# A state-space scan fused with a gated feed-forward layer: the first block's decays spread through four row groups of the array, and its dummy matmuls cut small

## The chip, the cores and the metric

The kernel runs on one core of one Trainium2 chip. The metric is the device time of the program in microseconds, as the median of several runs. Before the change it is 363.76 us (three runs, 362.59 to 363.86). The parts of the core are named as in the profile: PE is the matmul array (TensorE), PEld its weight loads, DVE is VectorE, ACT is ScalarE, POOL is GpSimd, and SP is SyncE, which here only issues transfers. A name with q behind it (SPq, ACTq) is the engine's instruction queue.

## The reference

Inputs: x (4 batches, 8 heads, 768 positions, 32 channels), decays a (4, 8, 768), B and C (4, 8, 768, 16), and three weight matrices. The first part is a chunked linear scan with a state of 16 by 32 for each batch and head; the second is a gated feed-forward layer on the result.

```python
log_a = np.log(np.clip(a, 1e-06, 1.0))
for c in range(nc):
    cum = np.cumsum(la, axis=-1)
    L = np.exp(cum[:, :, :, None] - cum[:, :, None, :]) * causal
    M = np.einsum('bhin,bhjn->bhij', Cc, Bc) * L
    y_intra = np.einsum('bhij,bhjd->bhid', M, xc)
    y_inter = np.einsum('bhin,bhnd->bhid', Cc, state) * np.exp(cum)[:, :, :, None]
    y[:, :, sl] = y_intra + y_inter
    state = decay_full[:, :, None, None] * state + np.sum(Bx, axis=2)
x = y.transpose(0, 2, 1, 3).reshape(3072, 256)
g = x @ w_gate
out = (g / (1 + np.exp(-g)) * (x @ w_val)) @ w_out
```

## The kernel before

**Tiling.** The 768 positions are cut into six blocks of 128 positions for all four batches at once (512 tokens a block), and each block into two pieces (q) of 64 positions, which are the scan's chunks. For each block k the kernel makes the decays L[k] (128 partitions are piece and position j; columns are batch, head and 65 positions i), the decays E[k] for the carried state, the scores S, the mixed matrix M (S times L, written over L), the sums st for the new state, the values y, and the state T. Then y is the input of the feed-forward layer: gate and value products gv in 12 steps of 128 columns of the hidden layer, silu and product (sg), and the output product po. Block 0 runs its gv in full float32 (two matmul records for one matmul, as for all float32 matmuls here); later blocks use weights split in a high and a low part, which VectorE and ScalarE make from the raw 64-bit weights during block 0 (tiles wg0 to wg11, wo0 to wo5: r raw, w rounded, h high, l low).

**Decays of block 0.** For blocks 1 to 5 the decays are clipped by GpSimd for all blocks at once, written to DRAM and loaded back with a broadcast. Block 0 cannot wait for that. `load_rows` (L239) loads its decays as 8 rows of 520 columns (rows[:, 0] for L, 8 rows that are piece and batch; rows[:, 1] for E, 8 rows that are heads). VectorE clips both (`clip_rows`, L298). `spread` (L303) copies the right rows to all 128 partitions with a float32 matmul by a matrix of zeros and ones, pick (loaded from `sel`, L876 to L879, one 8 x 128 matrix for each of the four batches and one for E). A spread covers half the columns (260), so there are eight for L and two for E; each writes a bank of PSUM in the pool `ps_at`, and VectorE scans it from there into L or E (`scan_spread`, L309), multiplying along the positions. The scan starts anew where the tile dj (for E: dn) has a one; dj is copied from the constants `cs` by ScalarE.

**What follows in block 0.** The scores (`scores_of`, L364) need C with heads kept apart (Cz, ScalarE). They are 32 small float32 matmuls on pieces of the array, 32 rows by 64 columns, and write four banks of the pool `ps_mm`. VectorE weighs B by the decays (`weigh_b`, tile xb) and mixes S with L (`mix`). PE then runs the sums st (`sums_of_pieces`), the values y (`values`, two groups of four heads), and the carried products (`carried`, tile y from bc and T). VectorE and ScalarE copy y to xf, and the first gv starts.

**Dummies.** `idle` (L621) issues a matmul of the tile unit (ones, bfloat16, 128 x 384) into a PSUM tile rest that nobody reads: eight before the first spread, eight before the carried products and eight between these and the first gv. Each has its own weight load.

**What sets the order.** Every step is added to a planner (`Plan`, L44) with an engine, a cost, a rank and what it needs; the planner runs through its own clock and issues each engine's instructions in the order it finds. `plan.follow` (L822 to L827) pins part of block 0's order by hand. The engines' queues are strictly in that order; `Ordered` (L182) pins it in the program. DMA issues sit in the queues of SP and ACT: SP issues rows, pick, the inputs of the clipping (tile all), the raw weights and later loads; ACT issues cs, then bc (B and C, 512 KB) and xb (x and B, 768 KB) of block 0.

Of the kernel before, what the change touches and what calls it, by code (L numbers as in the profile page):

```python
# [9 lines left out]
F32 = mybir.dt.float32  # L10
F32R = mybir.dt.float32r
BF16 = mybir.dt.bfloat16
# [31 lines left out]
class Plan:  # L44
# [156 lines left out]
def scan_moe_kernel(ctx: ExitStack, tc, aj, an, bc, xb, wgv, wo, cst, sel, out):  # L201
    nc = tc.nc
    PSUM = bass.MemoryType.PSUM
    te, ve, se, ge, sp = (
        Ordered(tc, e) for e in (nc.tensor, nc.vector, nc.scalar, nc.gpsimd, nc.sync)
    )

    def pool(name, bufs, stack=ctx, **kw):
        return stack.enter_context(tc.tile_pool(name=name, bufs=bufs, **kw))

    const = pool("const", 1)
    wts = pool("wts", 1)
    att = pool("att", 1)
    moe = pool("moe", 2)
    raw = pool("raw", RAW)
    dram = pool("dram", 1, space=bass.MemoryType.DRAM)
    ps_mm = pool("ps_mm", 4, space=PSUM)
    ps_at = pool("ps_at", 4, space=PSUM)

    cs = const.tile([P, CST], F32, name="cs")  # L220
    eye, hm, blk = cs[:, 0:W], cs[:, W : W + 2], cs[:, W + 2 : W + 2 + 2 * D]
    dj = const.tile([P, H, W], F32, name="dj")
    dn = const.tile([P, BATCH * K, W], F32, name="dn")
    unit = const.tile([P, 3 * P], BF16, name="unit")
    pick = const.tile([H, BATCH + 1, P], F32, name="pick")

    const.tile([P, 48], F32, name="gap")
    att.tile([P, 16], F32, name="gap2")
# [1 line left out]
    bl = [dict(y={}) for _ in range(NB)]  # L230
# [7 lines left out]

    def load_rows():  # L239

        t = moe.tile([H, 2, T + 32], F32, tag="xl", name="rows")
        t = bl[0]["rows"] = t[:, :, : H * W]
        sp.dma_start(t[:, 0], aj[0].rearrange("q (b c) -> (q b) c", b=BATCH))
        sp.dma_start(t[:, 1], an[0])

    def load_aj(k):
        t = bl[k]["L"]
# [14 lines left out]
    def new_decays(k):  # L262
        bl[k]["L"] = att.tile([P, BATCH * H, W], F32, tag="L", name=f"L{k}")
        bl[k]["E"] = att.tile([P, BATCH, K, W], F32, tag="E", name=f"E{k}")
# [22 lines left out]
    def clip(t):  # L287
        ve.tensor_scalar(t, t, 1e-6, 1.0, ALU.max, ALU.min)
# [7 lines left out]
        ve.tensor_tensor_scan(t, t, d, 0.0, ALU.mult, ALU.add)  # L296

    def clip_rows(i):  # L298
        clip(bl[0]["rows"][:, i].rearrange("p (g t) -> p g t", t=W)[:, :, 1:])

    HALF = H // 2 * W

    def spread(b, i):  # L303

        t = bl[0]["spread", b, i] = ps_at.tile([P, HALF], F32, tag="at", name=f"a{b}_{i}")
        r = bl[0]["rows"][:, b // BATCH, HALF * i : HALF * i + HALF]
        te.matmul(t, pick[:, b], r, start=True, stop=True)

    def scan_spread(b, i):  # L309
        if b < BATCH:  # L310
# [72 lines left out]
    def last(k, q):  # L383
        return k == NB - 1 and q == K - 1
# [82 lines left out]
    xh, xl = {}, {}  # L467
# [151 lines left out]
    rest = {}  # L619

    def idle(n, i):  # L621

        if not i:
            rest[n] = ps_at.tile([P, 3 * P], F32, tag="at", name=f"rest{n}")
        te.matmul(rest[n], unit[:, :P], unit, start=True, stop=True)


    load_rows()
    se.dma_start(cs, cst)
    sp.dma_start(pick, sel)  # L630
    new_decays(0)
    warm = const.tile([P, 1], F32, name="warm")
    ve.memset(unit, 1.0)
    ve.memset(warm, 1.0)
    se.activation(warm, warm, AF.Silu)
    load_bc(0)
# [4 lines left out]
    def do(f, *a):  # L641
        return lambda *e: f(*a, *e)
# [6 lines left out]
    add = plan.add  # L649

    GV, PO, ATT, FIRST, PACE0 = 2.82, 1.41, 5.0, 16.0, 3.5
    begin, begin_sum, t = {}, {}, FIRST
# [7 lines left out]
    def due(k, f=0):  # L660

        return begin[k] + f * (GV if k else PACE0)

    def due_sum(k, f):
        return begin_sum[k] + f * PO
# [5 lines left out]

    for n, ranks in enumerate(IDLE):
        for i, r in enumerate(ranks):
            need = [("idle", n, i - 1)] if i else IDLE_AFTER[n]
            takes = [] if i else [("at", ("rest", n))]
            add("PE", 0.16, do(idle, n, i), r, need, takes=takes, uses=[("rest", n)], gives=("idle", n, i), kind="r")


    for i in range(NW):
        r = due(0, i) - 1.0 if i < NF else due_sum(0, 2 * (i - NF)) - 1.0  # L680
# [7 lines left out]
        if i < NF:  # L688
            r = due(1, i) - LATER
# [10 lines left out]
    for k in range(NB):  # L700
        r = due(k)
# [9 lines left out]
        q = ("SP", 0.48) if k else ("-", 0.0)  # L711
# [7 lines left out]
        if not k:  # L719
            add("-", 0.0, lambda: None, -9, takes=[("x", "rows")], gives="rows", lag=0.2)  # L720
            for i in range(2):
                add("DVE", 0.35, do(clip_rows, i), -9 + i, ["rows"], gives=("clip", i))
            for b in range(BATCH + 1):
                r = z + 0.5 + b if b < BATCH else -1.3
                for i in range(2):
                    t = ("spread", b, i)
                    add("PE", 0.45, do(spread, b, i), r + 0.5 * i, [("clip", b // BATCH), "pick"], takes=[("at", t)], uses=[t, "rows"], gives=t, kind="s")
                    need = [t, ("decays", 0), "dj"] + ([("scan0", b)] if i else [])
                    done = ("scan0", b) if not i else ("L", 0, b) if b < BATCH else ("E", 0)
                    add("DVE", 0.63, do(scan_spread, b, i), r + 0.5 * i, need, uses=[t], gives=done)  # L730
        else:
            add("SP", 0.96, do(load_aj, k), FETCH["aj"] if k == 1 else z - 12, ["written", ("decays", k), *late], gives=("aj", k), lag=4.3)
            add("SP", 0.48, do(load_an, k), FETCH["an"] if k == 1 else z - 9, ["written", ("decays", k), *late], gives=("an", k), lag=1.1)
            for b in range(BATCH):
                add("DVE", 1.14, do(scan_j, k, b), z + 0.5 + b, [("aj", k)], gives=("L", k, b), slack=1.0)
            add("DVE", 1.17, do(scan_n, k), z + 6, [("an", k)], gives=("E", k), slack=1.0)
# [27 lines left out]
        for g in range(0 if k else 2):  # L764
            need = [("M", 0, p) for p in (2 * g, 2 * g + 1)]
# [22 lines left out]
    for k in range(NB):  # L788
        xs = [(t, k, i) for t in ("xh", "xl") for i in range(2 * K)]
        for f in range(NF):  # L790
            r = due(k, f)
            need = [*xs, ("wh", f), ("wl", f)]
            c = 1.4
            if not k:
                need = [("round", f), *(("xf", i) for i in range(2 * K))]
                c = 1.72
# [11 lines left out]
        for n, (m, t, fs) in enumerate(sums_of(k)):  # L808
            b = ("po", k, m, t)
            need = [x for f in fs for x in (("hl", k, f), ("wh", NF + f // 2), ("wl", NF + f // 2))]  # L810
            need += [prev] if prev else []
            prev = (*b, fs)
            r = due_sum(k, fs[0]) + n * 0.01
            c = 0.7 * len(fs) * (t[1] - t[0]) / T
            add("PE", c, do(project, k, m, t, fs), r, need, takes=[] if fs[0] else [("mm", b)], uses=[b, *(("h", k, f) for f in fs)], gives=prev, kind="r")
            if fs[-1] == NF - 1:
                o = ("ob", k, m, t)
                c = 0.6 * (t[1] - t[0]) / T
                add([("Act", c), ("DVE", c)], None, do(drain, k, m, t), r + 0.5, [prev], takes=[("ob", o)], uses=[b, o], gives=o)
                add("SP", 0.48, do(store, k, m, t), r + 2, [o], uses=[o], gives=("stored", k, m, t), lag=0.9)  # L820
    halves = [(b, i) for b in range(BATCH) for i in range(2)]
    plan.follow([  # L822
        *(("spread", b, i) for b, i in halves), *(("S", 0, b) for b in range(BATCH)),
        *(("spread", BATCH, i) for i in range(2)), *(("st", 0, b) for b in range(BATCH)), ("idle", 1, 0),
    ])
    plan.follow([("raw", i) for i in range(NW)])
    plan.follow([("L", 0, b) if i else ("scan0", b) for b, i in halves] + [("M", 0, p) for p in range(NP)] + [("scan0", BATCH), ("E", 0), ("ce", 0)])  # L827
# [1 line left out]
    plan.issue()  # L829


CST = W + 2 + 2 * D
NA = NB * K * BATCH * H // P
IDLE = [-9.0] * 8, [-1.2 + 0.1 * i for i in range(8)], [0.5 + 0.5 * i for i in range(8)]
IDLE_AFTER = [], [("S", 0, BATCH - 1)], [("y", 0)]
FETCH = dict(aj=10.0, an=29.0, bc=12.0, xb=31.0)
LATER = 3.0
LEAD = {1: -30.0, 2: -44.0, 3: -44.0}
# [54 lines left out]
```

## Time and profile before

| what | value |
|---|---|
| median of three runs | 363.76 us |
| the profiled execution, own time | 362.51 us |
| its span in the profile | 360.7 us |
| PE busy | 353.0 us (98%) |
| DVE busy | 238.6 us (66%) |
| ACT busy | 115.7 us (32%) |
| instructions | 7359 |

The time of the profiled execution is 1.8 us longer than its span, for what lies around the profiled instructions. Start times are counted from the span's start. The chain of waits follows the work that ended last backwards from the last instruction; "issue" in it is time in which the engine waited for nothing that the profile shows. In timeline rows the columns are start, length, engine, line (always the helper's, L190), operation, output and inputs, shapes, count, and in brackets the idle time before and what ended it. A matmul is shown with rows*columns of the array that it uses. In a tile's rows the three durations are the shortest, the median and the longest in ns. Rows of DMA queues give packets, MB and the share of 16 engines' time; rows of DMA issues give KB and the median time from issue to landing.

### The profile page before, as it was taken

What the parts mean: (1) busy time and instruction counts of PE and PEld (TensorE: products, weight loads), DVE (VectorE), ACT (ScalarE), POOL (GpSimd) and SP (SyncE); (2) the same over time, 40 slices, a digit from 0 to 9 for tenths busy, and PEclk for the clock granted to TensorE, in tenths of its full rate; (3) what the DMA queues carried; (4) which work ended last, traced back from release to release, by engine and by line L of the source; (5) the groups of instructions that cost most, each with busy time, mean ns of one, the idle gap of its engine ahead of it and who ended that gap; (6) DMA issues with size and microseconds to landing.
All of it is one profiled execution on the core that took longest, in us unless ns stands there. A gap on an engine that the chain in (4) does not pass through costs nothing.

```text
span 360.7 us, 7359 instructions
## 1 busy us (share of the span) xinstructions
PE 353.0 (98%) x3184; PEld 268.8 (75%) x3184; DVE 238.6 (66%) x446; ACT 115.7 (32%) x209; POOL 2.3 (1%) x7
## 2 busy tenths in 40 slices
PE   7989999999999999999999999999999999999996
PEld 4744444588878788887888887788877788888895
DVE  4869999989999967568263868255768250466230
ACT  3168575541353540222130322140313130311221
POOL 2000000000000000000000000000000000000000
PEclk9999999999999999999999999999999999999999
DMA  7928933290000085100056100046100000100001
GB/s 252 355 83 208 404 142 109 61 211 24 2 0 4 5 202 147 58 3 0 4 160 135 59 2 2 2 144 152 59 2 2 2 2 0 58 2 0 0 2 58
DMA packets 8456, 28.09 MB, mean 78 GB/s; under 512 B 976, under 2 KB 1872, under 8 KB 7784
## 3 DMA queue, kind: packets, MB, share of 16 engines
q1 hardware_dynamic: 7992, 26.25, 24.5%
q10 hardware_dynamic: 432, 1.38, 1.1%
q8 instruction: 25, 0.41, 0.4%
q14 instruction: 7, 0.06, 0.1%
HBM read 24.28 MB, written 3.35 MB: 77 GB/s over the span
## 4 chain that ended last, share of the span: by engine, by line
PE 90%; DVE 7%; issue 2%; DMA 1%; SPq 0%; ACT 0%; DVEq 0%; ACTq 0%
PE gv L190 51%; PE po L190 28%; PE y L190 4%; PE a L190 3%; PE S L190 2%; DVE L L190 1%; PE st L190 1%; DVE sg L190 1%; PE rest L190 1%; DMA pick<-in_sel 1%; DVE wg9w L190 1%; DVE wg7w L190 1%; DVE wg8w L190 1%; DVE T L190 1%; DVE wg5w L190 0%
## 5 line engine op out<-in xcount | busy, mean ns | idle before, releaser
L190 DVE TENSOR_TENSOR sg<-gv,sg 128x512 f32<-128x512 f32 x72 | 49.7, 690 | 69.1 <-PE gv L190 68.3
L190 ACT ACTIVATE sg<-gv 128x512 f32<-128x512 f32 x72 | 43.0, 597 | 111.9 <-PE gv L190 111.8
L190 DVE TENSOR_TENSOR hh<-sg,hh 128x512 fp32r<-128x512 f32 x72 | 49.4, 692 | 12.1 <-ACT hh L190 10.7
L190 ACT CAST hh<-sg 128x512 fp32r<-128x512 f32 x39 | 24.1, 622 | 37.1 <-PE po L190 15.2
L190 DVE TENSOR_TENSOR_SCAN L<-L,dj 128x520 f32<-128x520 f32 x20 | 23.8, 1228 | 14.1 <-DMA L<-clipped 14.1
L190 ACT COPY ob<-po 128x512 f32<-128x512 f32 (+1 forms) x13 | 7.2, 555 | 48.6 <-PE po L190 48.2
L190 DVE TENSOR_TENSOR L<-S,L 128x512 f32<-128x512 f32 x24 | 15.4, 688 | 1.5 <-PE S L190 1.5
L190 PE MATMUL po<-hh,wo0h 128*128 128x512 f32 (+1 forms) x52 | 15.7, 385 | 0.0
L190 PE MATMUL po<-hh,wo5h 128*128 128x512 f32 (+1 forms) x52 | 15.2, 375 | 0.0
L190 PE MATMUL po<-hh,wo2h 128*128 128x512 f32 (+1 forms) x52 | 15.2, 375 | 0.0
L190 PE MATMUL po<-hh,wo3h 128*128 128x512 f32 (+1 forms) x52 | 15.2, 375 | 0.0
L190 PE MATMUL po<-hh,wo4h 128*128 128x512 f32 (+1 forms) x52 | 15.1, 373 | 0.0
L190 PE MATMUL po<-hh,wo1h 128*128 128x512 f32 (+1 forms) x52 | 15.1, 373 | 0.0
L190 DVE CAST hh<-sg 128x512 fp32r<-128x512 f32 x33 | 14.1, 428 | 1.0
L190 PEld LDWEIGHTS y<-L,xb 64*32 64x32 f32 x768 | 9.1, 111 | 6.3 <-issue 3.6
L190 PE MATMUL y<-L,xb 64*32 64x64 f32 x768 | 11.1, 238 | 1.8 <-issue 1.8
L190 PEld LDWEIGHTS po<-hh,wo4h 128*128 128x128 f32 x52 | 9.5, 188 | 1.7
L190 PEld LDWEIGHTS po<-hh,wo1h 128*128 128x128 f32 x52 | 9.5, 188 | 1.7
L190 PEld LDWEIGHTS po<-hh,wo2h 128*128 128x128 f32 x52 | 9.4, 188 | 1.8
L190 PEld LDWEIGHTS po<-hh,wo3h 128*128 128x128 f32 x52 | 9.4, 188 | 1.8
L190 PEld LDWEIGHTS po<-hh,wo5h 128*128 128x128 f32 x52 | 9.4, 188 | 1.7
L190 PEld LDWEIGHTS po<-hh,wo0h 128*128 128x128 f32 x52 | 9.2, 188 | 2.0 <-issue 0.2
(272 smaller groups left out, 722.0 us busy)
## 6 DMA issues: line engine op xcount, KB each, us to landing
L<-clipped SPq DMA_DIRECT2D x10, 520.0 KB, 8.3
xb<-in_xb SPq DMA_DIRECT2D x5, 768.0 KB, 10.4
out<-ob SPq DMA_DIRECT2D x11, 256.0 KB, 2.0
bc<-in_bc SPq DMA_DIRECT2D x5, 512.0 KB, 3.4
E<-clipped SPq DMA_DIRECT2D x5, 260.0 KB
xb<-in_xb ACTq DMA_DIRECT2D x1, 768.0 KB
bc<-in_bc ACTq DMA_DIRECT2D x1, 512.0 KB, 4.2
wg0r<-in_wgv SPq DMA_DIRECT2D x1, 512.0 KB, 7.8
```

Of the source, the lines that this page charges most:

```text
L190: ins = getattr(self.engine, name)(*a, **k)
```

## The change

The four batches' rows of L are put at partitions 0, 32, 64 and 96 (two rows each, for the two pieces), so that each batch's spread uses a row group of its own. The rest of these 128 rows is filled with ones by VectorE ahead of the load, which is now two transfers, one for each piece. The matrix that spreads them is the same for all batches; it lies in 128 more columns of the constants `cs` (the view pick). Only E keeps a small matrix of its own, pick_n. The four first halves go to the banks of `ps_mm` (which the scores use after them), the four second halves to `ps_at`. A dummy is now 64 columns instead of 384, and each planned dummy step issues four: 40 before the first spreads, 24 between the first and the second halves, 28 before the carried products, 32 before the first gv. Costs and the pinned order follow.

```diff
-    unit = const.tile([P, 3 * P], BF16, name="unit")
-    pick = const.tile([H, BATCH + 1, P], F32, name="pick")
+    pick = cs[:, CST - P :]
+    unit = const.tile([P, P], BF16, name="unit")
+    pick_n = const.tile([H, P], F32, name="pick_n")
...
-        t = moe.tile([H, 2, T + 32], F32, tag="xl", name="rows")
+        t = moe.tile([P, 2, T + 32], F32, tag="xl", name="rows")
         t = bl[0]["rows"] = t[:, :, : H * W]
-        sp.dma_start(t[:, 0], aj[0].rearrange("q (b c) -> (q b) c", b=BATCH))
-        sp.dma_start(t[:, 1], an[0])
+        ve.memset(t[:, 0], 1.0)
+        to = t[:, 0].rearrange("(b r) c -> b r c", b=BATCH)
+        for q in range(K):
+            sp.dma_start(to[:, q], aj[0, q].rearrange("(b c) -> b c", b=BATCH))
+        sp.dma_start(t[:H, 1], an[0])
...
     def spread(b, i):
-        t = bl[0]["spread", b, i] = ps_at.tile([P, HALF], F32, tag="at", name=f"a{b}_{i}")
-        r = bl[0]["rows"][:, b // BATCH, HALF * i : HALF * i + HALF]
-        te.matmul(t, pick[:, b], r, start=True, stop=True)
+        where, tag = (ps_mm, "mm") if first(b, i) else (ps_at, "at")
+        t = bl[0]["spread", b, i] = where.tile([P, HALF], F32, tag=tag, name=f"a{b}_{i}")
+        half = slice(HALF * i, HALF * i + HALF)
+        if b < BATCH:
+            own = slice(32 * b, 32 * b + K)
+            te.matmul(t, pick[own], bl[0]["rows"][own, 0, half], start=True, stop=True)
+        else:
+            te.matmul(t, pick_n, bl[0]["rows"][:H, 1, half], start=True, stop=True)
...
-            rest[n] = ps_at.tile([P, 3 * P], F32, tag="at", name=f"rest{n}")
-        te.matmul(rest[n], unit[:, :P], unit, start=True, stop=True)
+            rest[n] = ps_at.tile([P, P], F32, tag="at", name=f"rest{n}")
+        for _ in range(4):
+            te.matmul(rest[n][:, :REST], unit, unit[:, :REST], start=True, stop=True)
...
     load_rows()
+    ve.memset(unit, 1.0)
     se.dma_start(cs, cst)
-    sp.dma_start(pick, sel)
+    sp.dma_start(pick_n, sel)
     new_decays(0)
-    ve.memset(unit, 1.0)
...
+REST = 64
-IDLE = [-9.0] * 8, [-1.2 + 0.1 * i for i in range(8)], [0.5 + 0.5 * i for i in range(8)]
-IDLE_AFTER = [], [("S", 0, BATCH - 1)], [("y", 0)]
+IDLE = [-9.0] * 10, [-4.0] * 6, [-1.0 + 0.1 * i for i in range(3)], [-1.0 + 0.1 * i for i in range(4)], [0.5 + 0.5 * i for i in range(8)]
+IDLE_AFTER = [], [("spread", BATCH - 1, 0)], [("S", 0, BATCH - 1)], [("vals", 1)], [("y", 0)]
...
-    halves = [(b, i) for b in range(BATCH) for i in range(2)]
+    halves = [(b, i) for i in range(2) for b in range(BATCH)]
     plan.follow([
-        *(("spread", b, i) for b, i in halves), *(("S", 0, b) for b in range(BATCH)),
-        *(("spread", BATCH, i) for i in range(2)), *(("st", 0, b) for b in range(BATCH)), ("idle", 1, 0),
+        *(("spread", b, 0) for b in range(BATCH)), *(("idle", 1, i) for i in range(len(IDLE[1]))),
+        *(("spread", b, 1) for b in range(BATCH)), *(("S", 0, b) for b in range(BATCH)),
+        *(("spread", BATCH, i) for i in range(2)), *(("st", 0, b) for b in range(BATCH)), ("idle", 2, 0),
     ])
...
+    cst[:, CST - P :] = (p % 32)[:, None] == (p // Q)[None, :]
+    sel = (np.arange(H)[:, None] == p // N).astype(np.float32)
```

On PE, between the first dummies and the scores, this stood before (a0_1 is the spread of batch 0, second half; S0_0 the scores of block 0, first bank):

```order
L190 MATMUL rest0_105<-unit_81 128x384
L190 MATMUL a0_0_125<-rows_86,pick_82 128x260
L190 MATMUL a0_1_127<-rows_86,pick_82 128x260
L190 MATMUL a1_0_130<-rows_86,pick_82 128x260
...
L190 MATMUL a3_1_147<-rows_86,pick_82 128x260
L190 MATMUL S0_0_149<-Cz0_134,bc0_97 64x128
```

In the changed program the same place on PE reads so (24 dummies rest1 stand where two of their rows are shown):

```order
L190 MATMUL rest0_107<-unit_81 128x64
L190 MATMUL a0_0_159<-rows_87,cs_78 128x260
L190 MATMUL a1_0_161<-rows_87,cs_78 128x260
L190 MATMUL a2_0_164<-rows_87,cs_78 128x260
L190 MATMUL a3_0_166<-rows_87,cs_78 128x260
L190 LDWEIGHTS unit_81
L190 MATMUL rest1_168<-unit_81 128x64
...
L190 MATMUL a0_1_198<-rows_87,cs_78 128x260
L190 MATMUL a1_1_201<-rows_87,cs_78 128x260
L190 MATMUL a2_1_203<-rows_87,cs_78 128x260
L190 MATMUL a3_1_206<-rows_87,cs_78 128x260
L190 MATMUL S0_0_209<-Cz0_186,bc0_99 64x128
```

The halves of a batch no longer follow each other; the four first halves come together, then dummies, then the four second halves. Behind the scores PE's order is the old one as far as the first gv, with 28 and 32 dummies in the two places that had eight; in gv step 7 of block 0, block 1's sums moved between its two matmul groups and block 1's scores behind both.

At the start of VectorE's queue (the row with 128x520 fills the ones, the rows TENSOR_SCALAR clip, the later ones scan):

```order
-L190 MEMSET unit_81 128x384
-L190 MEMSET warm_93 128x1
-L190 TENSOR_SCALAR rows_86<-rows_86 8x8x64 x2
-L190 SCALAR_TENSOR_TENSOR L0_91<-a0_0_125,dj_79 128x260
-L190 SCALAR_TENSOR_TENSOR L0_91<-a0_1_127,dj_79 128x260
...
+L190 MEMSET rows_87 128x520
+L190 MEMSET unit_81 128x128
+L190 MEMSET warm_86 128x1
+L190 TENSOR_SCALAR rows_87<-rows_87 128x8x64
+L190 TENSOR_SCALAR rows_87<-rows_87 8x8x64
+L190 SCALAR_TENSOR_TENSOR L0_95<-a0_0_159,dj_79 128x260
+L190 SCALAR_TENSOR_TENSOR L0_95<-a1_0_161,dj_79 128x260
```

The memset of unit, for which the first dummies wait, now stands behind that of rows. At the start of SP's queue:

```order
-L190 DMA rows<-in_aj 8x520
+L190 DMA rows<-in_aj 4x520 x2
 L190 DMA rows<-in_an 8x520
-L190 DMA pick<-in_sel 8x640
+L190 DMA pick_n<-in_sel 8x128
 L190 DMA all<-in_aj 128x195
 L190 DMA all<-in_an 128x195
```

The first two transfers of rows wait for VectorE's memset, and all other transfers of SP stand behind them.

More of the change, by code (lines that the diff above doesn't have):

```diff
@@ L298, in clip_rows, with first @@
     def clip_rows(i):
-        clip(bl[0]["rows"][:, i].rearrange("p (g t) -> p g t", t=W)[:, :, 1:])
+        t = bl[0]["rows"][:H, 1] if i else bl[0]["rows"][:, 0]
+        clip(t.rearrange("p (g t) -> p g t", t=W)[:, :, 1:])
     HALF = H // 2 * W
+    def first(b, i):
+        return b < BATCH and not i
     def spread(b, i):
-        t = bl[0]["spread", b, i] = ps_at.tile([P, HALF], F32, tag="at", name=f"a{b}_{i}")
-        r = bl[0]["rows"][:, b // BATCH, HALF * i : HALF * i + HALF]
-        te.matmul(t, pick[:, b], r, start=True, stop=True)
+        where, tag = (ps_mm, "mm") if first(b, i) else (ps_at, "at")
[6 more added lines that the diff above has]
+            te.matmul(t, pick_n, bl[0]["rows"][:H, 1, half], start=True, stop=True)
     def scan_spread(b, i):
@@ L623, in idle @@
         if not i:
-            rest[n] = ps_at.tile([P, 3 * P], F32, tag="at", name=f"rest{n}")
-        te.matmul(rest[n], unit[:, :P], unit, start=True, stop=True)
+            rest[n] = ps_at.tile([P, P], F32, tag="at", name=f"rest{n}")
+        for _ in range(4):
+            te.matmul(rest[n][:, :REST], unit, unit[:, :REST], start=True, stop=True)
+    warm = const.tile([P, 1], F32, name="warm")
     load_rows()
+    ve.memset(unit, 1.0)
     se.dma_start(cs, cst)
-    sp.dma_start(pick, sel)
+    sp.dma_start(pick_n, sel)
     new_decays(0)
-    warm = const.tile([P, 1], F32, name="warm")
-    ve.memset(unit, 1.0)
     ve.memset(warm, 1.0)
@@ L675, in scan_moe_kernel @@
             takes = [] if i else [("at", ("rest", n))]
-            add("PE", 0.16, do(idle, n, i), r, need, takes=takes, uses=[("rest", n)], gives=("idle", n, i), kind="r")
+            add("PE", 0.12, do(idle, n, i), r, need, takes=takes, uses=[("rest", n)], gives=("idle", n, i), kind="r")
     for i in range(NW):
@@ L726, in scan_moe_kernel @@
                     t = ("spread", b, i)
-                    add("PE", 0.45, do(spread, b, i), r + 0.5 * i, [("clip", b // BATCH), "pick"], takes=[("at", t)], uses=[t, "rows"], gives=t, kind="s")
+                    add("PE", 0.25 if first(b, i) else 0.45, do(spread, b, i), r + 0.5 * i, [("clip", b // BATCH), "pick" if b == BATCH else "cs"], takes=[("mm" if first(b, i) else "at", t)], uses=[t, "rows"], gives=t, kind="s")
                     need = [t, ("decays", 0), "dj"] + ([("scan0", b)] if i else [])
@@ L829, in scan_moe_kernel @@
     plan.issue()
-CST = W + 2 + 2 * D
+CST = W + 2 + 2 * D + P
+REST = 64
 NA = NB * K * BATCH * H // P
-IDLE = [-9.0] * 8, [-1.2 + 0.1 * i for i in range(8)], [0.5 + 0.5 * i for i in range(8)]
-IDLE_AFTER = [], [("S", 0, BATCH - 1)], [("y", 0)]
+IDLE = [-9.0] * 10, [-4.0] * 6, [-1.0 + 0.1 * i for i in range(3)], [-1.0 + 0.1 * i for i in range(4)], [0.5 + 0.5 * i for i in range(8)]
+IDLE_AFTER = [], [("spread", BATCH - 1, 0)], [("S", 0, BATCH - 1)], [("vals", 1)], [("y", 0)]
 FETCH = dict(aj=10.0, an=29.0, bc=12.0, xb=31.0)
@@ L872 @@
     cst[:, W : W + 2] = odd[:, None] == np.arange(2)[None, :]
-    cst[:, W + 2 :] = odd[:, None] == (np.arange(2 * D) // D)[None, :]
-    sel = np.zeros((H, BATCH + 1, P), np.float32)
-    row = np.arange(H)[:, None]
-    for b in range(BATCH):
-        sel[:, b] = row == BATCH * (p // Q) + b
-    sel[:, BATCH] = row == p // N
+    cst[:, W + 2 : CST - P] = odd[:, None] == (np.arange(2 * D) // D)[None, :]
+    cst[:, CST - P :] = (p % 32)[:, None] == (p // Q)[None, :]
+    sel = (np.arange(H)[:, None] == p // N).astype(np.float32)
     ins = dict(aj=aj, an=an, bc=bc, xb=xb, wgv=wgv, wo=wo, cst=cst, sel=sel)
```

## Prediction

> **What bounds the kernel now.** I read the chain of waits first, since it says which work ended last in each stage (start, length, what; us).
>
> ```profile
> 1.54 3.17 DMA pick<-in_sel
> ...
> 4.84 7.27 PE a L190 x16
> 12.11 1.94 PE S L190 x64
> 14.05 2.03 PE a L190 x4
> 16.08 0.90 PE st L190 x47
> ...
> 18.06 1.76 issue
> 19.82 1.17 PE y L190 x63
> 20.99 2.19 PE rest L190 x8
> 23.18 0.62 PE y L190 x32
> 23.80 1.41 PE rest L190 x8
> 25.21 6.88 PE gv L190 x16
> ...
> 59.06 0.71 DVE wg9w L190
> 59.91 3.67 PE gv L190 x8
> ```
>
> From 25.21 on PE streams nearly without a gap; the gap that counts is at 59, where gate/value step 9 waits for VectorE. So a change to the first 25 us is worth the shift of the first gv, less what VectorE's queue adds at 59. Before 25.21 the path is: a load, eight spreads (16 records), scores, a stop of 1.76 in which PE waited for nothing shown, values, dummies, carried products, dummies.
>
> VectorE's timeline over the same stretch:
>
> ```profile
> 2.40 0.89 DVE L190 TENSOR_SCALAR rows<-rows 8x512 f32<-8x512 f32 x2 [1.13 <-DMA rows<-in_aj]
> 6.16 1.49 DVE L190 TENSOR_TENSOR_SCAN L<-a,dj 128x260 f32<-128x260 f32 x2 [2.87 <-PE a L190]
> ...
> 11.28 0.70 DVE L190 TENSOR_TENSOR_SCAN L<-a,dj 128x260 f32<-128x260 f32 x1 [0.17 <-PE a L190]
> 11.90 0.67 DVE L190 TENSOR_TENSOR xb<-xb,L 128x128 f32<-128x128 f32 x3
> ...
> 14.11 1.29 DVE L190 TENSOR_TENSOR L<-S,L 128x512 f32<-128x512 f32 x2 [0.93 <-PE S L190]
> 15.32 0.28 DVE L190 TENSOR_TENSOR xb<-xb,L 128x128 f32<-128x128 f32 x1
> 15.51 1.28 DVE L190 TENSOR_TENSOR L<-S,L 128x512 f32<-128x512 f32 x2
> 16.71 0.69 DVE L190 TENSOR_TENSOR_SCAN E<-a,dn 128x260 f32<-128x260 f32 x1
> 17.32 0.40 DVE L190 TENSOR_SCALAR wg0w<-wg0w 128x512 f32<-128x512 f32 x1
> ```
>
> Each scan of 0.70 is preceded by 0.17 idle for PE: the spreads, at 7.27/8 = 0.9 each, pace the scans. Unpaced, a scan takes 0.61 from start to start (16.71 to 17.32). Then M (the mixing at 14.11) waits 0.93 for the scores, which stand behind all spreads.
>
> **The change part by part.**
>
> *Start of the spreads.* VectorE now fills rows with ones before the rows may be loaded.
>
> ```profile
> 0.73 0.70 POOL L190 MEMSET dn<- 128x520 f32 x2 [0.29 <-POOLq L882]
> 0.74 0.41 SPq L190 DMA_DIRECT2D rows<-in_aj  x1
> 0.89 0.38 DVE L190 MEMSET unit<- 128x384 bf16 x1 [0.89 <-PEq L882]
> ```
> ```profile
> all<-in_aj SPq DMA_DIRECT2D x1, 97.5 KB, 3.9
> ```
>
> 384 columns took 0.38, and on GpSimd 520 columns with a small one 0.70: I take 0.55 (0.4 to 0.7), from 0.89 to 1.44. The first rows load issues at 1.5 instead of 0.74, which is the place of pick before (1.54), and the second half 0.41 later, at 1.9. Rows took 1.66 from issue to use (0.74 to 2.40), pick 3.17, the next load in the queue 3.9: issued beside the large bc load, a small load waits. So the second half lands at 3.6 to 5.8; I take 4.9, as for pick. All later loads on SyncE (rows an, pick_n, the clipping's inputs, the weights) move by about 1 us as well; the first of these weights is used by gv at 25, and pick_n by the fifth spread after the scores, so that costs nothing. The constants (cs) double in width but are issued as before, ahead of bc. Clipping adds 0.42 and the hand-over 0.13: spreads begin at 5.45, not 4.84; with the old 1.32 from spread to scan (4.84 to 6.16), the first scan begins at 6.8: 0.6 lost.
>
> *Four spreads side by side.* Whether row groups run at once shows in the scores, four row groups by two column halves:
>
> ```profile
> 12.04 2.01 PE L190 MATMUL S<-Cz,bc 32*64 32x128 f32 x64
> ```
> ```profile
> L190 PE MATMUL S<-Cz,bc x64: 416/416/471, 12.0 to 13.6; 32*64 32x128 f32 x64
> ```
>
> 64 records of 416 ns in 2.01 leave (2.01 - 0.42)/63 = 25 ns from one to the next, so they overlap. Four spreads then cost about what one did: 1.32 less the hand-over, 1.2 us on PE, instead of 4 x 0.87 = 3.5.
>
> *The dummies.* What does a dummy of 64 columns cost?
>
> ```profile
> 22.18 0.15 PEld L190 LDWEIGHTS <-unit 128*128 128x128 bf16 x1 [0.17 <-issue]
> 22.50 0.29 PEld L190 LDWEIGHTS <-unit 128*128 128x128 bf16 x2 [0.17 <-issue]
> ...
> 23.74 1.47 PE L190 MATMUL rest<-unit 128*128 128x384 bf16 x8
> ```
> ```profile
> L190 PE MATMUL rest<-unit x24: 326/502/527, 1.3 to 24.9; 128*128 128x384 bf16 x24
> ```
> ```profile
> L190 PEld LDWEIGHTS y<-L,xb x53: 102/106/107, 63.5 to 64.0; 64*32 64x32 f32 x53
> ```
> ```profile
> 63.51 0.86 PE L190 MATMUL y<-L,xb 64*32 64x64 f32 x64
> ```
>
> ```profile
> PEclk9999999999999999999999999999999999999999
> ```
>
> Old dummies stand 0.32 apart up to 22.50 (0.83 ns a column) and (1.47 - 0.33)/7 = 0.163 apart from 23.74: the array runs at half speed until about 22.5, though the granted clock reads full throughout. By columns alone, 64 cost 53 ns cold and 27 warm. But each brings a weight load, recorded at 150. The nearest row with loads as frequent is y: 64 records in 0.86 are 10 ns apart, over eight tiles 81 ns for each tile, less than the 106 of its load, so loads overlap. I take 70 cold and 50 warm (bounds 53 to 150, 27 to 100). Then the first 40 cost 2.8 and run from 1.65 to 4.5, hidden before the spreads; 24 cost 1.7; 28 cost 2.0; the last 32 cost 1.6.
>
> *The sum to the values.* First four scans 6.8 to 9.3 (0.63 each). PE: spreads done 6.65, 24 dummies to 8.35, the second four give their first scan at 8.35 + 1.32 = 9.7. Four scans and three weighings (0.67) end at 12.85, where M stood at 14.11: 1.25 gained. Scores run from 9.4 (their banks come free with the first scans) to 11.4, no longer last. The fourth weighing ends at 14.35, sums and values start at 14.45 instead of 16.08 (the two spreads for E, at 14.05, no longer stand in front), and after 18.06 - 16.08 = 1.98 the second values could start at 16.45; M is through at 15.55. Before it was 19.82.
>
> *The stop of 1.76.* I put it to PE's code load:
>
> ```profile
> q8 instruction: 1, 0.02, 13.1%
> ```
> ```profile
> q8 instruction: 1, 0.02, 15.6%
> ```
> ```profile
> q8 instruction: 25, 0.41, 0.4%
> ```
>
> The first row is the stretch 17.0 to 17.5, the second 20.5 to 21.0, the third the page's total for the span. PE stopped after some 442 records (matmuls and loads: 16 dummies, 40 of spreads, 128 scores, 128 sums, 130 values) and resumed 2.4 after the packet. The second packet began 0.9 after the resumption, so I assume that entering one piece orders the next and that this takes some 3.5 us in all; 256 records of small matmuls run in 2. With 112 more records ahead of the scores, the first order now falls into the scores, near 10, and is back by about 14, needed at 15.6: that stop goes. The next order at 15.6 is back near 19.2 and needed about 18.3, amid the 28 dummies: 0.9 comes back (0 to 1.8).
>
> *The sum to the end.* Second values 16.45 + 1.17, dummies 2.0, stop 0.9, carried 0.62: 21.1 instead of 23.80, so 2.7 earlier. The last 32 dummies end at 22.7, first gv 2.5 earlier. VectorE's queue starts 2.7 earlier, but the planner now puts one low-part subtraction ahead of weight 9:
>
> ```profile
> 32.61 0.69 DVE L190 TENSOR_TENSOR sg<-gv,sg 128x512 f32<-128x512 f32 x1 [0.62 <-ACT wg6w L190]
> ...
> 63.40 0.70 DVE L190 TENSOR_TENSOR wg1l<-wg1w,wg1h 128x512 fp32r<-128x512 f32 x1
> ```
>
> That is 0.6 more before the wait at 59 (it stood at 63.4), some of which idle time like the 0.62 at 32.61 can take. I take 2.4 saved. The profiled execution took 362.51 (span 360.7): 360.1. The runs were 362.59, 363.76 and 363.86; where the array speeds up by luck of timing, some runs lose more. I add 0.5 for the median: **360.6**, with 359.0 to 361.9 for this case.
>
> **The rivals.**
>
> *Dummies bound by their weight loads* (slower). If each takes its load's 150 cold and 100 warm: the first 40 end at 7.65, 24 take 3.6, M starts at 17.0, second values at 20.6, 28 take 4.2, 32 take 3.2, gv at 29.8 instead of 25.2: **367**. It turns from gain to loss at about 100 ns a dummy. For it: the load record; against: the y row, and eight large dummies that hid theirs. [...] Chance 0.11.
>
> *The array stays cold into gv.* If small dummies do not raise the clock, gv runs at half speed until it has raised it itself; before, about 2.7 us of steady work did that (19.82 to 22.5). Half of 2.7 lost, perhaps twice: **362.0** to 363.3. [...] For: gaps between small dummies; against: PE is busy from 14.45. Chance 0.12.
>
> *Code load as long as before*: 1.8 instead of 0.9: **361.6**; it fetches amid weight traffic. Chance 0.10.
>
> *The change doesn't do what it says*: the four spreads run one after another. 3.5 instead of 1.2, second scans at 11.9 paced by 0.87, M 1.7 later than before, the stop gone: **363.0**. Against: the scores' 25 ns. Chance 0.07.
>
> **How the numbers follow.** Forecast 0.60. About 0.5% (1.8 us) is what a measurement here can tell from no change, so faster ends at 361.9. The forecast, most of the code case and a little of the clock case are faster: 0.69. The rest of these and the serial case: 0.20. Load-bound dummies: 0.11. The range 358.6 to 363.4 takes in a landing at 3.6 to 5.8 and the cheap dummies below, and all rivals but the slow one.
>
> **What would show it.** Right: rows' first load issued near 1.5, spreads from about 5.4 with four starts together, scans closing up to 0.61 to 0.7, M near 12.9, no 1.76 stop before the second values, gv near 22.7. Wrong: dummies more than 100 ns apart, spreads 0.87 apart, gv records of 0.86, or a VectorE wait near 57 of much over 1 us.

## The result, and the profile after

The kernel after takes 366.61 us (median of 6 runs, 365.34 to 367.65), the kernel before, run beside it, 363.17 (6 runs, 360.94 to 364.17): ratio 1.0101, 95% interval 1.006 to 1.0141. The forecast was 360.6, so faster; the change makes the kernel 1.0% slower. The profiled execution of after took 366.59 with a span of 364.8, which is 4.1 more than before's 360.7.

First the chain of waits of after (start, length, what; us).

```profile
1.43 4.02 DMA rows<-in_aj
...
8.74 1.24 PE a L190 x8
...
12.66 1.94 PE S L190 x64
...
17.89 1.89 issue
19.78 0.78 PE y L190 x36
...
21.77 0.59 PE rest L190 x9
22.37 1.42 issue
23.79 1.20 PE rest L190 x19
24.98 1.06 PE y L190 x32
26.05 1.82 PE rest L190 x32
27.86 2.50 PE gv L190 x5
```

Three things stand in it that the forecast did not have. The spreads begin at 8.74, not 5.45. The stop of 1.76 is still there (now 1.89), and it ends at 19.78, almost where it ended before (19.82), although everything ahead of it has changed. And a second stop of 1.42 has come, amid the dummies. Both stops are "issue": PE waits for nothing that the profile shows. From the end of the first stop on, the bill is: values and sums 1.99 instead of 1.17 (more of them were left over), dummies 1.79 instead of 2.19, the second stop 1.42, carried products 1.06 instead of 0.62, last dummies 1.82 instead of 1.41. Together that is 2.69 more, from a start that is 0.04 earlier: gv enters the chain at 27.86 instead of 25.21.

VectorE's timeline shows when the rows could be used and what follows from it.

```profile
0.91 0.49 DVE L190 MEMSET rows<- 128x520 f32 x1 [0.91 <-PEq L895]
...
8.25 0.75 DVE L190 TENSOR_SCALAR rows<-rows 128x512 f32<-128x512 f32 x2 [6.69 <-DMA rows<-in_aj]
10.06 4.38 DVE L190 TENSOR_TENSOR_SCAN L<-a,dj 128x260 f32<-128x260 f32 x7 [1.07 <-PE a L190]
...
15.56 1.26 DVE L190 TENSOR_TENSOR L<-S,L 128x512 f32<-128x512 f32 x2
```

Clipping waits 6.69 for the rows' load and begins at 8.25, where 4.9 was forecast. From there the steps are as forecast: the scans run at 4.38/7 = 0.63 each, and M starts 6.8 after the spreads (forecast 7.4). M at 15.56 is later than before's 14.11 because the rows are; run g1 below, with the rows at 4.28, has M at 11.60.

PE's timeline, the first dummies and gate/value step 9:

```profile
1.60 2.32 PE L190 MATMUL rest<-unit 128*128 128x64 bf16 x40 [1.60 <-DVE warm L190]
...
63.12 3.70 PE L190 MATMUL gv<-xf,wg9w 128*128 128x512 f32 x8 [0.83 <-DVE wg9w L190]
```

A cold dummy (one from before the array speeds up; in before, dummies of 384 columns stood 0.32 us apart up to 22.5 and 0.163 from 23.74 on) takes some 53 ns: 2.32 less one of about 0.24, over 39. Step 9 is at 63.12 instead of 59.91, so 3.2 of the 4.1 are there by then: 2.65 from the start of gv, and 0.56 between that and the weight that PE waits for VectorE to make. The last 0.9 is there by 112, where the third block's scores wait 0.61 for VectorE; in before they do not.

The prediction put the first stop down to the load of PE's own instructions. The profile has a queue "q8 instruction", 26 packets and 0.43 MB in after. I read each of its packets as one piece of the program; the point in PE's work where, by this reading, one piece ends and the next is needed is called a border here. This is that queue in after, in the stretch 17.0 to 17.5 (packets, MB, share of the 16 engines):

```profile
q8 instruction: 1, 0.02, 12.3%
```

The issue of xb in ScalarE's queue:

```profile
1.98 0.45 ACTq L190 DMA_DIRECT2D xb<-in_xb  x1
```

And of the rows and the first of the late weights in SyncE's:

```profile
1.43 1.28 SPq L190 DMA_DIRECT2D rows<-in_aj  x2
...
10.89 0.47 SPq L190 DMA_DIRECT2D wg2r<-in_wgv  x1
```

The packet moves at 17.27, as late as before (17.35). If the trace's records of PE (matmuls, weight loads and semaphore steps) are counted in order, the first stop stands behind record 449 in both kernels, and after's second behind record 705, which is 256 further. Before reaches 705 in gv, at 31, and does not stop there.

### The profile page after: what moved, and what is told of

It reads as the page before. It is cut to its first block, busy times and chain, and to the rows that moved or that the text cites. A ratio compares the mean times of both kernels' runs of the same rounds, so it can differ in the third digit from the quotient of the medians.

```text
span 364.8 us, 7565 instructions
## 1 busy us (share of the span) xinstructions
PE 350.5 (96%) x3284; PEld 269.5 (74%) x3284; DVE 238.3 (65%) x446; ACT 116.2 (32%) x210; POOL 2.3 (1%) x7
## 4 chain that ended last, share of the span: by engine, by line
PE 76%; DVE 14%; DMA 5%; issue 4%; ACT 0%; SPq 0%; DVEq 0%; ACTq 0%
PE gv L190 40%; PE po L190 27%; PE y L190 4%; DVE sg L190 3%; DVE L L190 3%; DMA L<-clipped 3%; PE S L190 2%; PE rest L190 1%; PE a L190 1%; DMA rows<-in_aj 1%; PE st L190 1%; DMA wg0r<-in_wgv 1%; DVE T L190 1%; DVE wo1w L190 1%; DVE wg9w L190 1%
## 5 line engine op out<-in xcount | busy, mean ns | idle before, releaser
L190 ACT CAST hh<-sg 128x512 fp32r<-128x512 f32 x41 | 25.4, 622 | 45.3 <-PE po L190 15.6
L190 DVE CAST hh<-sg 128x512 fp32r<-128x512 f32 x31 | 13.2, 427 | 1.0
```

The source lines that it names most:

```text
L190: ins = getattr(self.engine, name)(*a, **k)
```

## The experiments

There were three theories. **Code**: PE's instructions come in pieces of 256 records, the distance between after's two stops; the small dummies (124 matmuls and as many loads, where before had 24) bring the borders forward in the work, and a border that is reached before its piece is there stops PE. **Late rows**: the landing at 8.25 cost the time. **Clock**: small dummies leave the array at half speed. The first four runs were made to tell them apart. Each ratio below is to the kernel before as it ran beside that run; differences between two experiments compare medians that were not all taken side by side.

**e1: rows first.** This is after without the fill of rows, so that their loads can be issued first of all; the rows are clipped where they lie.

```
-        ve.memset(t[:, 0], 1.0)
...
+        for own in [slice(0, H)] if i else [slice(32 * b, 32 * b + K) for b in range(BATCH)]:
+            clip(t[own, i].rearrange("p (g t) -> p g t", t=W)[:, :, 1:])
```

> The kernel after, without the fill of rows with ones; the eight rows that are used are clipped by four instructions of two partitions each, so the two loads of the rows are issued first of all, near 0.75 and 1.2 instead of 1.43 and 2. Late-rows theory (the rows' landing at 8.25 is what cost the time): rows land at 3 to 5, the first spreads start at 5 to 6 instead of 8.73, M starts near 13, and the first gv comes 2.5 to 3.5 us sooner than in the kernel after (24.2 to 25.2 instead of 27.7): 363.0 to 364.0 against 366.6. Code theory (PE's instructions arrive in pieces of 256 records; the stops sit at records 449 and 705): the spreads also come sooner, but the stops stay at the same records; the second one amid the dummies before the carried products is still there with 1 to 1.5 us, and the first one ends when its piece has been fetched, no sooner than about 2.4 us after record 193 is passed and later if the weights are on the move. If the first stop still ends near 19.8, the time stays within 1 us of 366.6.

364.34 us; ratio to before 1.0052 (1.0022 to 1.0083). The chain of e1:

```profile
5.69 2.58 PE a L190 x5
...
17.79 0.73 PE rest L190 x9
18.52 4.13 issue
```

The spreads start 3 us sooner than in after, the scores 1.7 sooner (10.95), but gv only 1.1. The stop at record 449 is gone, which neither theory had expected, and the one at 705 has grown to 4.13. So late rows alone do not explain the loss: most of what was gained ahead was lost at the border.

**e2: large dummies in fewer records.** This is after with dummies of 384 columns again, one for each planned step and 21 in all.

```
+        te.matmul(rest[n], unit[:, :P], unit, start=True, stop=True)
...
+REST = 3 * P
...
+IDLE = [-9.0] * 7, [-4.0] * 4, [-1.0 + 0.1 * i for i in range(2)], [-1.0 + 0.1 * i for i in range(3)], [0.5 + 0.5 * i for i in range(5)]
```

> The kernel after with the old dummies of 384 columns: 7, 4, 2, 3 and 5 of them in place of 40, 24, 12, 16 and 32 of 64 columns, so the array is kept busy as long, but 103 matmuls and 103 weight loads fewer pass through PE, 110 of these records ahead of the scores. Code theory: the stop at record 449 falls later in the work (behind the first values, as in the kernel before) and ends near 19.8; the stop of 1.42 amid the dummies before the carried products goes, since record 705 falls into gv; first gv at 25 to 25.7 instead of 27.7, time 363 to 364.3. Late-rows theory: rows still land near 8.2 and M near 15.5, so nothing is gained: 366 to 367. Clock theory (small dummies leave the array cold): the full clock is recorded near 22.5 to 24 again instead of 28.3, and the carried products and first gv are 1.2 us shorter, with or without the second stop: 365.

358.4 us (358.25 to 358.79); ratio 0.9899 (0.9866 to 0.9933). That is some five us better than the code theory had expected. PE's timeline of e2:

```profile
6.61 1.25 PE L190 MATMUL a<-rows,cs 2*128 2x260 f32 x8 [2.32 <-DVE rows L190]
...
18.77 0.69 PE L190 MATMUL y<-bc,T 32*64 32x64 f32 x32
...
20.21 3.60 PE L190 MATMUL gv<-xf,wg0w 128*128 128x512 f32 x8
```

The first of the late weights in SyncE's queue of e2:

```profile
12.01 0.47 SPq L190 DMA_DIRECT2D wg2r<-in_wgv  x1
```

There is no stop at all: not at 705 (in gv now, at 27.5), as expected, but not at 449 (16.1) either, whose piece moved at 13.23 instead of 17.27. The rows were usable at 6.13; xb was issued at 2.92 here, behind both loads of the rows. So e2 differs from after in two things, fewer records and rows that are 2.1 sooner; f3 below tells them apart.

**e3: both.** The edits of e1 and e2 together.

> Both edits on the kernel after: the rows loaded first and clipped in place without the fill, and the old dummies of 384 columns in fewer records. Code theory: one stop only, at record 449 behind the first values; record 193 is passed some 3 us sooner than in the kernel after, so the piece arrives sooner and the stop is shorter than 1 us or gone; first gv at 22.5 to 24.5, time 360.5 to 362.5. Late-rows theory: first gv 3 us sooner than in the kernel after whatever the dummies: 363.5, the same as with the rows alone. If the fetch is bound by the weights' traffic and not by when it is ordered, the stop ends near 19.8 as before and the time is that of the big dummies alone, 363 to 364.

363.47 us (359.52 to 364.74); ratio 1.0008 (0.9974 to 1.0041). The chain of e3:

```profile
16.48 0.20 PE st L190 x12
16.68 2.51 issue
```

Two gains together gave none: the stop at 449 is back with 2.51, because its piece moved at 16.91. Here SyncE had issued wg2 at 10.85, and PE passed record 150 at 11.80; in e2 it was the other way round, 12.01 and 11.60. That gave a new theory, **queue**: the piece is ordered some 50 records ahead of the border before (193, so near record 150), and if the weights wg2 to wg6 (2.5 MB) have been issued by then, it waits for them.

**e4: small dummies only.** This is before with 64, 28 and 32 dummies of 64 columns.

```
+        for _ in range(4):
+            te.matmul(rest[n][:, :REST], unit, unit[:, :REST], start=True, stop=True)
...
+IDLE = [-9.0] * 16, [-1.2 + 0.1 * i for i in range(7)], [0.5 + 0.5 * i for i in range(8)]
```

> The kernel before, with only its dummies changed: 64, 28 and 32 of 64 columns in place of 8, 8 and 8 of 384 columns, as many as the kernel after has in all, the first 64 in the idle time before the spreads; rows, spreads and the order of all other work are as before. Code theory: the first stop begins 112 records sooner in the stream, amid the sums or first values, and still ends near 19.8; a second stop of 1 to 1.9 us shows between 21 and 25, at record 705; first gv at 26.5 to 27.7 instead of 24.9, time 364.3 to 366 against 362.5. Late-rows theory: rows land as before at 2.4, so the time stays at 362 to 363.3. Clock theory: the full clock comes later than 22.5 and gv's first step is slower, 0.5 to 1.2 us more, with no second stop.

362.19 us; ratio 1.0001 (0.9967 to 1.0035). The chain of e4:

```profile
19.16 0.59 PE rest L190 x9
19.76 1.97 issue
```

The stop at 705 came, at the same dummy as in after and e1 (behind nine of the 28). The one at 449 went, so one stop was traded for another of about its size, and the time that the code theory gave (364.3 to 366) was missed.

The next four runs try the queue theory; f3 tries the count of records again. In the other three a small DMA that needs VectorE's fourth weighing is put ahead of the weights wg2 to wg6 on SyncE, so that they are issued later; the planned steps for these five loads then issue nothing:

```
+        if k == 0 and b == BATCH - 1:
+            hold()
...
+    def hold():
+        sp.dma_start(held, bl[0]["Bj"][:1, BATCH - 1, :16])
+        for i in range(2, 7):
+            w_fetch(i)
```

**f1: before, weights held.** This is before with that edit and no other.

> The kernel before, with one small DMA added on SyncE ahead of the loads of wg2 to wg6: it writes sixteen numbers of xb, after VectorE's fourth weighing, to a scratch tensor that nothing reads. SyncE therefore issues the five weights (2.5 MB) from about 16 on instead of from 8.17. Order and form of all other instructions are as before. Queue theory (a piece of PE's instructions that is ordered after the weights have been issued waits until they are through; one that is ordered ahead of them comes in 1.2 us): the second piece, ordered near record 150 at 13.2, moves at about 14.4 instead of 17.35, the stop of 1.76 at record 449 goes, gv starts near 23.1 instead of 24.9, time about 361 against 363. Fixed-delay theory (the piece needs some 3.5 to 4 us from its order at record 193, whatever the traffic): stop and time stay, 362.5 to 363.5. If the late weights starve gv, it is slower than before and gv2 waits for VectorE's wg2w.

359.73 us; ratio 0.9923 (0.9878 to 0.9968). SyncE's queue of f1:

```profile
15.96 0.25 SPq L190 DMA_DIRECT2D held<-xb  x1
16.26 0.33 SPq L190 DMA_DIRECT2D wg2r<-in_wgv  x1
```

The chain of f1:

```profile
18.40 0.89 PE y L190 x62
19.28 1.57 PE rest L190 x8
...
22.89 5.16 PE gv L190 x12
```

The instruction queue of f1 in the stretch 15.5 to 16.0:

```profile
q8 instruction: 1, 0.02, 12.0%
```

The piece moved at 15.57 instead of 17.35 and the stop is gone; gv starts 2.3 sooner. Nothing else was changed, so the weights ahead of the piece were the cause of the stop in the kernel before. The fixed delay, which my prediction had taken, is refuted.

**f2: e3, weights held.** The same edit on the kernel of e3.

> The kernel of e3 (rows first, old dummies in fewer records) with the weights wg2 to wg6 held back by the same small DMA behind the fourth weighing, near 14.7 instead of 10.85. Queue theory: the second piece, ordered near 11.8, moves near 13 instead of 16.91; the stop of 2.51 at record 449 goes; gv starts near 20.5 and the time is that of e2, 358 to 359.3, in every run. Fixed-delay theory: the stop stays, 362.5 to 364.

359.48 us; ratio 0.9903 (0.9878 to 0.9928). No stop (the piece moved at 13.23, not 16.91). PE's timeline of f2:

```profile
20.18 3.67 PE L190 MATMUL gv<-xf,wg0w 128*128 128x512 f32 x8
```

gv starts where it does in e2. The time was expected at 358 to 359.3 in every run; the median and seven of the ten runs (to 360.96) lie above that.

**f3: e2 with 98 more records.** Only the first seven dummies are replaced, by eight small ones each.

```
+        if n:
+            te.matmul(rest[n], unit[:, :P], unit, start=True, stop=True)
+        else:
+            for _ in range(8):
+                te.matmul(rest[n][:, :64], unit[:, :P], unit[:, :64], start=True, stop=True)
```

> The kernel of e2 (the fastest so far, no stop), with only its first seven dummies of 384 columns replaced by 56 of 64 columns: 98 records more, all in the idle time before the rows land (3.0 us of work from about 1.9, spreads start at 6.6). If only the array's idle time counts, nothing changes: 358.4. Count theory: record 705 now lies where record 607 was, near 17.5, amid the dummies before the carried products; its piece is ordered near record 400, at about 15, behind the weights, moves near 20 and can be used near 22.5. A stop of 4 to 5 us shows there, gv starts near 25, time 362.3 to 363.6. The stop at record 449 stays away, since its piece is now ordered even earlier.

363.27 us; ratio 1.0029 (0.9986 to 1.0072). The chain of f3:

```profile
17.94 0.27 PE y L190 x7
18.20 3.53 issue
```

Its windows (stretch; its length; PE's busy time with the number of instructions; granted clock; DMA share; GB/s):

```profile
18.00:20.00 2.00, 0.20 (x7) 1.00 1.03 418
20.00:22.00 2.00, 0.26 (x9) 0.69 0.76 301
22.00:24.00 2.00, 2.00 (x29) 0.50 0.19 35
24.00:26.00 2.00, 2.00 (x5) 0.50 0.92 312
26.00:28.00 2.00, 2.00 (x4) 0.60 0.74 173
```

These dummies lie wholly in idle time, and yet the kernel loses 4.9 us against e2, from 13 us later on: record 705 is reached at 17.99, and its piece moves at 19.25 (from 18 to 20 the DMA moves 418 GB/s). The rows were usable even sooner than in e2 (5.38 against 6.13), so the added records alone are to blame. The windows show the second price of a stop: the granted clock, full from 18 to 20, falls to 0.50, and the first gv step takes 5.31 instead of the 3.60 of e2.

**f4: after, weights held.** The same edit on the kernel after.

> The kernel after with the weights wg2 to wg6 held back by the small DMA behind the fourth weighing, about 16.7 instead of 10.89. Queue theory: the second piece, ordered near 11.3, moves near 12.5 instead of 17.27 and the stop of 1.89 at record 449 goes; but the third piece, ordered near 17.2, now stands behind all the held weights (to about 22), so the stop amid the dummies, reached near 20.2, grows from 1.42 to 3 to 5 us. gv starts at 26.5 to 28.5, the time is 364.5 to 367.5: the gain of the one stop is lost in the other. If stops only depend on the number of records, the first stop stays and the time is 366.6.

361.67 us; ratio 0.9956 (0.9931 to 0.9982). The chain of f4:

```profile
20.02 0.54 issue
...
21.45 0.62 PE y L190 x32
22.08 1.04 PE rest L190 x32
```

The first stop is gone, as expected (piece at 13.81). The second did not grow, against the expectation: its piece moved at 18.23. I had put its order behind wg2; PE passed record 400 at 17.00, just ahead of wg2 at 17.13, which would put it ahead, but no view shows the order itself. So one DMA takes 4.9 us off the kernel after (366.61 to 361.67), though its rows are still late (8.04). The small dummies are warm here (the first record of a full clock stands at 20.95): 32 in 1.04, 33 ns each, and the carried products take the old 0.62.

**g1: after, bc and xb behind the rows.** SyncE issues these two loads, behind the rows, in place of ScalarE.

```
-        (sp if k else se).dma_start(t, bc[k])
+        sp.dma_start(t, bc[k])
```

The load of xb is changed likewise.

> The kernel after with the loads of bc and xb issued by SyncE, behind the rows and pick_n (near 3.6 and 4), in place of ScalarE (1.61 and 1.98, while the rows' second piece is issued near 2.1). If the rows came late because bc and xb went ahead of their second piece, they now land near 4 instead of 8.2, the spreads start at 4.5 to 5.2 and M at 12 to 13 instead of 15.56. Whether that pays is the other question. Count theory: no stop at record 449 (its piece is ordered near 8, ahead of the weights), but record 705 is reached near 17 and its piece, ordered near 14 behind the weights, comes near 20 to 22: a stop of 3.5 to 5 there, gv at 24 to 26.5, time 362.5 to 365. Late-rows theory: the 3.5 us pass through to gv, time 363.

363.51 us; ratio 1.0004 (0.998 to 1.0029). VectorE's timeline of g1:

```profile
4.28 0.75 DVE L190 TENSOR_SCALAR rows<-rows 128x512 f32<-128x512 f32 x2 [2.73 <-DMA rows<-in_aj]
...
11.60 1.26 DVE L190 TENSOR_TENSOR L<-S,L 128x512 f32<-128x512 f32 x2
```

The chain of g1:

```profile
15.97 0.59 PE rest L190 x9
16.56 4.44 issue
```

The rows are usable at 4.28 instead of 8.25, so bc and xb, which after issued ahead of the rows' second load, were what delayed them. M starts 4 us sooner than in after and 2.5 sooner than in before, better than my forecast. But it buys 3.1 against after, not 4, and nothing against before, because PE then stops for 4.44 at 705. (At 449, reached at 13.6, it lost 0.04.)

**g2: e2, bc and xb behind the rows.** The same edit on the kernel of e2.

> The kernel of e2 (old dummies of 384 columns, no stop; 358.4) with bc and xb issued by SyncE behind the rows. Rows land near 4 instead of 6.1 and the spreads start at 4.5 instead of 6.6. Both pieces of PE's instructions are still in time by the queue theory (the second ordered near 9.5, ahead of wg2; record 705 lies in gv, near 25, and its piece is usable by 22.5), so the 2 us pass through to gv (18 to 18.5) and, less what VectorE's queue takes at gate/value step 9, to the end: 356 to 357.3. If bc's later landing holds up Cz and the scores, or VectorE is the bound by now, the time stays at 358 to 358.6.

357.35 us (356.68 to 358.42); ratio 0.9835 (0.9799 to 0.9872). This is the lowest median, though it was not measured beside e2, and the two ranges overlap a little. PE's timeline of g2:

```profile
18.69 3.60 PE L190 MATMUL gv<-xf,wg0w 128*128 128x512 f32 x8
...
103.71 1.17 PE L190 MATMUL S<-Cz,bc 32*64 32x128 f32 x60 [1.33 <-DVE T L190]
```

There is no stop, and gv starts 1.5 sooner than in e2. Of this 0.9 is lost at 103.7, where the third block's scores wait 1.33 for VectorE, against 0.40 in e2: VectorE is the next bound there.

All kernels in one table, from the traces (us; "passed" and "reached" by PE's records, pieces by the start of the instruction packet; a dash is no stop):

| kernel | record 150 passed | wg2 issued | 2nd piece | 449 reached, stop | 3rd piece | 705 reached, stop | first gv | median |
|---|---|---|---|---|---|---|---|---|
| before | 13.20 | 8.17 | 17.35 | 17.75, 1.76 | 20.95 | 31.06, – | 25.05 | 363.2 |
| after | 11.30 | 10.89 | 17.27 | 17.58, 1.89 | 21.39 | 22.12, 1.42 | 27.68 | 366.6 |
| e1 | 9.59 | 10.95 | 10.79 | 15.81, – | 20.17 | 18.28, 4.13 | 26.54 | 364.3 |
| e2 | 11.60 | 12.01 | 13.23 | 16.10, – | 20.15 | 27.51, – | 20.21 | 358.4 |
| e3 | 11.80 | 10.85 | 16.91 | 16.37, 2.51 | 20.35 | 32.26, – | 24.75 | 363.5 |
| e4 | 8.66 | 9.61 | 12.62 | 17.19, – | 19.41 | 19.52, 1.97 | 25.59 | 362.2 |
| f1 | 13.54 | 16.26 | 15.57 | 18.07, – | 21.85 | 28.73, – | 22.72 | 359.7 |
| f2 | 11.81 | 15.42 | 13.23 | 16.31, – | 19.83 | 27.55, – | 20.18 | 359.5 |
| f3 | 8.60 | 12.04 | 11.68 | 14.69, – | 19.25 | 17.99, 3.53 | 24.16 | 363.3 |
| f4 | 11.10 | 17.13 | 13.81 | 17.32, – | 18.23 | 19.78, 0.54 | 22.95 | 361.7 |
| g1 | 7.34 | 11.53 | 11.52 | 13.62, 0.04 | 18.57 | 16.32, 4.44 | 24.80 | 363.5 |
| g2 | 9.79 | 11.53 | 11.58 | 14.29, – | 18.53 | 25.98, – | 18.69 | 357.4 |

In the three kernels in which wg2 was issued ahead of record 150, and only there, the second piece comes at about 17; in the nine others it comes at 10.79 to 15.57. A late piece does not wait until all five weights are through: in after it moved at 17.27, while wg4 to wg6 landed only at 19.51 to 22.02. Every stop stands at one of the same two records. From the start of a piece's packet to the end of its stop lie 2.28 to 2.51 in all nine stops of over 0.1.

## Why the prediction was wrong, step by step

- *Rows usable at 4.9 (3.6 to 5.8)*: wrong, 8.25. I took pick's landing as the nearest row; but in before xb was issued at 2.60, behind pick, and now at 1.98, while the rows were still being issued. g1, with bc and xb behind, gave 4.28. Getting the rows that much sooner was worth 3.1 there (366.61 to 363.51).
- *Four spreads at once, 1.2*: right, 1.24; the rival of four spreads one after another is out. *Dummies 70 ns cold, 50 warm*: both too dear, 53 and 33 (f4), within the bounds. The rival of dummies bound by their weight loads is out too; that its 367 lies near the measured 366.6 is chance. *From the spreads to M 7.4*: 6.8.
- *The stop of 1.76 goes, since its piece is ordered near 10 and back by 14*: **this is the step that failed.** I had the 256 records and an early order, but gave the piece a fixed time of some 3.5 us from order to use. It has none. In after PE passed record 150 at 11.30, when wg2 had been issued (10.89), and the piece moved only at 17.27, so the stop stayed at 1.89. f1 and f4 show the cause: with the weights held, the stop goes from before and from after alike. (A reading was off too: the 0.9 from the end of the stop to the next packet, read from a half-microsecond stretch, is 1.13, from 19.82 to 20.95.)
- *A second stop of 0.9 (0 to 1.8) amid the 28 dummies*: the place was right, the size 1.42. That the size fell within 0 to 1.8 is luck, since it came from the same fixed delay. The stop is the price of the added records: with e2's fewer ones there is none, with 98 hidden ones in f3 it is 3.53. And g1, the nearest run to what the forecast assumed (rows at 4.28, no first stop), stops here for 4.44 and takes 363.5; so the forecast would most likely have failed without the late rows too. The rival *code load as long as before* named the weight traffic as the reason, but only for this second stop and for 0.9 us more.
- *The array stays cold into gv* (rival, 0.12): it happened, but not for its reason. In f4 the same small dummies are warm; in after the carried products and 32 dummies take 1.22 more than in f4 (1.06 + 1.82 against 0.62 + 1.04), behind the two stops; in f3 a clock already granted falls across a stop, from 1.00 in 18 to 20 to 0.50 in 22 to 24. The trace's clock records say the same. They begin with the first full clock, and a stretch ahead of the first of them reads as full in the views, which is why the clock of before read full throughout, though its first record stands at 22.55. That first record stands at 17.24 to 19.59 in the four kernels without a stop, at 20.95 in f4, and at 22.55 to 28.29 in the six others whose stop came ahead of it. So here the stops kept the array cold, not the small dummies: with the same dummies the first record stands at 20.95 in f4 and at 28.29 in after. The clock is their second price.
- *VectorE 0.6 later at step 9, of which the sum counted 0.1* (2.5 to 2.4 saved): 0.56 was lost. The subtraction of wg1 does stand ahead of weight 9, but VectorE also idled 1.27 at 31.76 (in before 0.62 at 32.61), ahead of the product that follows the first gv step (3.98 long, in before 3.60), so the forecast's reason is only a part of it. The 0.9 more at 112 was not forecast; the wait is 0 in before, and I have not separated its cause.

No view of before shows the 256 records that the prediction used; the distance between after's two stops, 449 and 705, does. Four of the twelve kernels pass both records without a stop; in the eight others a stop costs 0.54 to 4.44 us. Counted on from the row of the first stop, 200 more records (100 matmuls and their loads) bring 705 from inside gv (31.06 in before) to ahead of it (22.12 in after).

What stays open: the record at which a piece is ordered is not shown. Record 150 is a fit; the one hard bound is e1, where the packet moved at 10.79, before record 166 began (10.88). From record 150 to the packet lie 1.2 us in e1, but 2.7 in f4, 4.0 in e4 and 4.2 in g1, in all of which wg2 was issued after that record; so the weights are not all that a piece can wait for. What the runs do show is that holding the weights back moves the piece forward (17.35 to 15.57 in f1, 16.91 to 13.23 in f2, 17.27 to 13.81 in f4) and ends the first stop. And each trace is one execution: e3's runs reach from 359.52 to 364.74, and five of the 31 runs of before that were made beside f1 to f4 lie at 358.81 to 360.85, inside f1's range (358.24 to 362.66). A piece that sometimes gets ahead of the weights would explain both, but the single traces do not show it.

## What to carry to other kernels

Count an engine's instructions, not only its time: here 98 more records in idle time brought record 705 ahead of gv, to 17.99, and cost 4.9 us (f3 against e2). So fill idle time with few wide instructions. If a stop shows no releaser, look at the instruction queue's packet and at which bulk loads were issued ahead of it: here one DMA of 64 bytes that held such loads back took 4.9 us off the kernel after (f4), while the rebuilt computation had made the kernel 1.0% slower. And time a small load by what else is issued in the same microsecond, not by where such a load landed before: the same rows were usable at 8.25 with bc and xb issued among their loads, at 4.28 with these behind them.

## What the hardware showed unexpectedly

- PE stopped behind the same records, 449 and 705, in all eight kernels in which it stopped, whatever the instructions were; it resumed 2.28 to 2.51 us after the packet of the missing piece started to move.
- Across one stop of 3.53 us a full clock already granted was lost, for some 6.8 us by the means of the windows (f3: 1.00 in 18 to 20, 0.69 in 20 to 22, 0.50 from 22 to 26, 0.60 in 26 to 28).
- A dummy of 128x64 with its own weight load went through every 53 ns cold (after, 40 in 2.32 us) and every 33 ns warm (f4, 32 in 1.04).
- Two small loads of 4 partitions, issued from 1.43 on, became usable between 4.28 (g1) and 8.25 (after), by whether two large loads were issued by ScalarE at 1.6 and 2.0 or by SyncE, behind them, at 3.6 and 4.0.
